# Attention into a two-layer MLP: a flag gathered behind the last matmul, the last output tile in two halves, no fillers behind transpositions

## The chip, the cores and the metric

The kernel runs on one core of a Trainium2 chip. A core has five engines that each work through a list of instructions in order and wait for one another by semaphores: TensorE (PE; its weight loads are shown apart as PEld), VectorE (DVE), ScalarE (ACT), GpSimd (POOL) and SyncE (SP, which here only starts transfers and takes branches). The metric is the device time of one execution in microseconds; lower is better.

## The reference

Attention with a causal window of 128 positions and four "sink" positions that every row sees, for 4 batches, 8 heads, 768 positions and 64 dimensions; its result, as rows of 512 per token, goes through an MLP.

```python
scores = np.matmul(q, k.transpose(0, 1, 3, 2)) / np.sqrt(D)
keep = (pos[None, :] < n_sink) | ((rel >= 0) & (rel < window))   # rel = row - column
a = softmax(np.where(keep, scores, -1e9))
x = np.matmul(a, v).transpose(0, 2, 1, 3).reshape(B * S, H * D)   # 3072 x 512
h = x @ w_in                                                       # 512 x 2048
out = np.maximum(0.01 * h, h) @ w_out                              # 2048 x 512
```

The two weights arrive as 64-bit floats, `n_sink` and `window` as 64-bit integers.

## The kernel before

The tokens are cut into NU = 8 units `u` of 384 tokens (half a batch, T = 3 tiles of 128). A unit has attention (four pairs of heads) and an MLP of NFC = 16 steps `fc`, one for each 128 of the 2048 inner columns. A step of the MLP is twelve matmuls for `h` (128x384, L511: four blocks of the inner dimension, each as three products, high with high, low with high and high with low, since both operands are split in two parts) and nine for the output of the step before (128x512, L537: three token tiles, three products each: `woh,gh`, `wol,gh`, `woh,gl`). Between them ACT makes 0.01`h` (L518), DVE the maximum `g` (L521), ACT the high part `gh` (L522), POOL the low part `gl` (L523). While a unit goes through its MLP, PE does the attention of the next unit in between.

The 16 weight tiles of each matrix come as 64-bit words. DVE turns each into a 32-bit float in three instructions of 512 columns (`di` or `do` at L166 and L168, then `wi` or `wo` at L170, with the letter i for `w_in` and o for `w_out`); ACT and POOL then make the two parts (L179, L180). The first three tiles are decoded during the attention of unit 0, the others in the MLP steps of unit 0.

PE's order is written out by hand (L570: the recorded order holds for PE alone). The order of the other engines is made by a scheduler that lays the instructions out on a modelled timeline, so it can change wherever the program changes. On PE, L253 (`keep_warm`) issues filler matmuls of 256 columns into the bank `h`, with zeros and a result that nobody reads: 17 at the start, and one behind the four transpositions of each tile of unit 0's attention (in `turn_native`, L309 to L322).

PSUM is cut into eight banks of 128x512: `s0`, `s1`, `o0`, `o1`, `o2`, `t`, `h`, `d`. The outputs of a unit are summed in `o0`, `o1`, `o2` over 16 steps. Step 1 puts its `h` into the bank `o2` (L506), so the first matmul that writes `o2` as an output has to wait until `g` of step 1 has been read from it.

The kernel is only valid for small `n_sink`, `window` and normal numbers. `needs_general` (L595 to L615) collects the conditions on DVE into one number for each partition (`one`, L609), turns them into a row on PE (`flag_t`, L610) and reduces that to a flag (L612, L614). It is called in the last unit (u = 7) in the pass of the loop for step 14, behind the outputs of step 13 and ahead of `h` of step 15. Each engine loads the flag (L749) and branches on it (L750); the general path behind the branch isn't taken with these inputs.

The last output tile is read from its bank by halves: the first 256 columns by ACT, the others by DVE (L549), each stored by its own queue (L550: ACT's and SP's). The 23 tiles before it are copied by DVE (L553) and stored on SP's queue (L554).

Of the kernel before, what the change touches and what calls it, by code (L numbers as in the profile page):

```python
# [9 lines left out]
F32 = mybir.dt.float32  # L10
# [8 lines left out]
ENG = mybir.EngineType  # L19
MANUAL = {ENG.PE}  # L20
P = 128
B, H, S, D = 4, 8, 768, 64
DM, DF = 512, 2048
# [3 lines left out]
NFC = DF // P  # L27
T = 3
NU = 2 * B
# [100 lines left out]
def fast_path(ctx, tc, cpool, qp, qk, vu, vs, wq, out, ident, lim, masks, wz, negm, wmin, wmax):  # L130
    nc = tc.nc
# [7 lines left out]
    def bank(tag, name):  # L139
        return psum.tile([P, 512], F32, tag=tag, name=name)  # L140
# [3 lines left out]
    anchor = [None]  # L144
# [38 lines left out]
    def fetch_check(n):  # L183
        k, fc = divmod(n, NFC)
        raw = iopool.tile([P, 512, 2], I32, tag="raw", name=f"craw{n}", bufs=3)
        nc.sync.dma_start(out=raw.rearrange("p f t -> p (f t)"), in_=wq[k, fc])
        checks.append((n, raw))
# [63 lines left out]
    def keep_warm(n):  # L251
        for _ in range(n):
            nc.tensor.matmul(warm[:, 0:2 * P], lhsT=wz[:, 0:P], rhs=wz, start=True, stop=True)  # L253
# [55 lines left out]
    def turn_native(u, pair, j, w, state):  # L309
        half = u % 2  # L310
        kn = KSL[half][j][1]
        tp = turn_bank(u, f"t{u}_{pair}_{j}")
        cols = (0, W1) if kn == W3 else (NSK,)
        m = P * len(cols)
        o0 = 2 * P * j if half else max(2 * j - 1, 0) * P
        for o in range(2):
            for c, a in enumerate(cols):
                nc.tensor.transpose(out=tp[:, o * m + c * P:o * m + (c + 1) * P], in_=w[:, o, a:a + P],  # L318
                                    identity=ident)
        if u == 0:  # L320
            keep_warm(1)
        nc.scalar.copy(out=state["pt"][:, :, o0:o0 + m], in_=tp[:, 0:2 * m].rearrange("p (o q) -> p o q", o=2))  # L322

    def turn_packed(u, pair, o, w, state):
# [170 lines left out]
    def mlp_stream():  # L495
        po = {}
        prev = None
        for step in range(NU * NFC + 1):
# [27 lines left out]
                yield u  # L526
            if prev is not None:
                v, f, gh, gl = prev
                if f == 0:
                    po = [bank(f"o{t}", f"o{v}_{t}") for t in range(T)]  # L530
                wh, wl = wts["o", f]
                order = [(t, c) for t in range(T) for c in range(2)] + [(t, 2) for t in range(T)]
                if f == NFC - 1 or step == 1:
                    order.sort()
                for i, (t, c) in enumerate(order):
                    tsl = slice(t * P, (t + 1) * P)
                    nc.tensor.matmul(po[t], lhsT=(gl if c == 2 else gh)[:, tsl], rhs=wl if c == 1 else wh,  # L537
                                     start=f == 0 and c == 0, stop=f == NFC - 1 and c == 2)
                    if i in (2, 5):
                        yield v  # L540
                    if f < NFC - 1 or c < 2:
                        continue
                    last = v == NU - 1 and t == T - 1
                    r0 = (v * T + t) * P
                    if last:
                        for i, (copy, queue) in enumerate(((nc.scalar.copy, nc.scalar), (nc.vector.tensor_copy, nc.sync))):
                            half = slice(256 * i, 256 * (i + 1))
                            ob = iopool.tile([P, 256], F32, tag="raw", name=f"ob{v}_{t}_{i}", bufs=3)
                            copy(out=ob, in_=po[t][:, half])  # L549
                            queue.dma_start(out=out[r0:r0 + P, half], in_=ob)  # L550
                    else:
                        ob = iopool.tile([P, 512], F32, tag="io", name=f"ob{v}_{t}", bufs=3)
                        nc.vector.tensor_copy(out=ob, in_=po[t])  # L553
                        nc.sync.dma_start(out=out[r0:r0 + P, :], in_=ob)  # L554
                yield v
            prev = cur
            if u == NU - 1 and fc == NFC - 2:
                flags.append(needs_general(tc, anchor[0], cpool, bank("t", "flag_t"), ident, lim, negm,
                                           wmin, wmax))
                tc.mark_branch_hint_location("general", engines=[ENG.PE, ENG.Activation, ENG.DVE, ENG.Pool])  # L560
            at = step - FIRST_CHECK
            if at >= 0:
                for _ in range(2 if checks else 0):
                    check_weights()
                while len(checks) < min(3, 2 * NFC - 2 * at):
                    fetch_check(2 * at + len(checks))

    steps = [NPAIR * (2 * T + 2 if native(u) else 2 * T + 4) for u in range(NU)]
    flags = []
    stream = attention_stream()  # L570
    ctx.enter_context(tc.manual_schedule(engines=MANUAL))
    done = 0
# [19 lines left out]
    return flags[0]  # L592


def needs_general(tc, after, pool, row, ident, lim, negm, wmin, wmax):  # L595
    nc = tc.nc
    bad = pool.tile([P, 6], F32, name="bad")
    deep = pool.tile([P, 1], F32, name="deep")
# [8 lines left out]
        nc.vector.tensor_scalar(out=bad[:, 3 + i:4 + i], in0=deep, scalar1=bound, scalar2=None, op0=op)  # L607
    one = pool.tile([P, 1], F32, name="one")
    nc.vector.tensor_reduce(out=one, in_=bad, axis=AX.X, op=ALU.max)  # L609
    nc.tensor.transpose(out=row[0:1, 0:P], in_=one, identity=ident)  # L610
    allp = pool.tile([1, 1], F32, name="allp")
    nc.vector.tensor_reduce(out=allp, in_=row[0:1, 0:P], axis=AX.X, op=ALU.max)  # L612
# [186 lines left out]
```

## Time and profile before

| | us |
|---|---|
| median of 3 runs | 706.63 (706.54 to 706.93) |
| the profiled execution | 705.64 |
| its span in the trace | 703.9 |
| PE busy in the span | 688.9 (98%) |
| DVE, ACT, POOL busy | 443.5, 325.9, 315.4 |

The profile is of one execution, 0.99 us under the median of the runs and with 1.74 us outside its span. Shares over the whole span say little here: PE is 98% busy, but the span has a start in which other engines work too, a long stretch of steps and an end, which have to be looked at one by one. Times in the rows are in us from the start of the span; a row with "x3" merges three instructions in a row, and the bracket behind it gives the idle time of the engine before it and what ended it. A matmul's length in the rows runs past the start of the next one, so the time that one costs in a row of matmuls is read from start to start. A "q" behind an engine's name (SPq) is its queue of instructions that aren't counted as busy.

### The profile page before, as it was taken

The numbers are of one execution on the slowest core, as the hardware profiler recorded it, in microseconds if no ns is written. First come the engines' busy times: TensorE is split into PE (matmuls) and PEld (weight loads), VectorE is DVE, ScalarE is ACT, GpSimd is POOL, SyncE is SP. The second block draws the span as 40 slices with busy tenths as digits, with TensorE's granted clock in tenths as the row PEclk, the third lists the DMA queues.
The fourth block names the chain that finished last, engine by engine and source line by source line (L and its number), as shares of the span: only waits on it lengthen the run. The fifth ranks groups of instructions, "written<-read, shape, count | busy, mean of one in ns | idle before, by whom it ended". The sixth has DMA issues, their size and how long they took to land.

```text
span 703.9 us, 11359 instructions
## 1 busy us (share of the span) xinstructions
PE 688.9 (98%) x3938; PEld 595.0 (85%) x3938; DVE 443.5 (63%) x1181; ACT 325.9 (46%) x855; POOL 315.4 (45%) x390
## 2 busy tenths in 40 slices
PE   8889999999999999999999999999999999999995
PEld 5568788889888889888888988888898888889994
DVE  5997879655566556465566655565556755377663
ACT  5865666545444444444454444444454443222221
POOL 4676776654443444444354444344444433122221
PEclk9999999999999999999999999999999999999999
DMA  6675665421223211131222222132112320068751
GB/s 222 215 241 180 194 199 174 152 67 50 80 61 116 73 53 49 59 117 51 80 80 71 77 73 69 46 114 64 59 60 80 102 71 31 1 207 281 245 179 48
DMA packets 29534, 77.28 MB, mean 110 GB/s; under 512 B 3488, under 2 KB 9120, under 8 KB 29472
## 3 DMA queue, kind: packets, MB, share of 16 engines
q1 hardware_dynamic: 29328, 76.38, 33.9%
q8 instruction: 32, 0.52, 0.3%
q14 instruction: 30, 0.25, 0.1%
q10 hardware_dynamic: 144, 0.13, 0.1%
HBM read 70.21 MB, written 6.29 MB: 109 GB/s over the span
## 4 chain that ended last, share of the span: by engine, by line
PE 90%; DVE 6%; ACT 1%; issue 1%; DMA 0%; DVEq 0%; ACTq 0%
PE h L511 37%; PE o L537 36%; PE acc L366 5%; PE s L282 5%; PE t L328 2%; PE acc L373 2%; PE s L277 1%; PE t L318 1%; ACT pk L291 1%; DVE pk L289 1%; DVE di L168 1%; DVE do L166 1%; DVE do L168 1%; DVE di L166 1%; PE sk L344 0%
## 5 line engine op out<-in xcount | busy, mean ns | idle before, releaser
L523 POOL TENSOR_TENSOR gl<-g,gh 128x384 fp32r<-128x384 f32 x127 | 136.5, 1075 | 226.3 <-ACT gh L522 222.3
L511 PE MATMUL h<-xh,wih 128*128 128x384 f32 x512 | 180.7, 353 | 0.3 <-DVE g L521 0.2
L511 PE MATMUL h<-xl,wih 128*128 128x384 f32 x512 | 172.2, 336 | 1.2 <-POOL xl L381 1.2
L511 PE MATMUL h<-xh,wil 128*128 128x384 f32 x512 | 172.4, 337 | 0.0
L537 PE MATMUL o<-wol,gh 128*128 128x512 f32 x384 | 152.9, 398 | 0.0
L537 PE MATMUL o<-woh,gh 128*128 128x512 f32 x384 | 151.6, 395 | 0.9 <-DVE g L521 0.7
L537 PE MATMUL o<-woh,gl 128*128 128x512 f32 x384 | 114.1, 398 | 0.0
L291 ACT ACTIVATE pk<-pk,negm 128x132 f32<-128x132 f32 (+1 forms) x192 | 81.5, 425 | 62.8 <-DVE negm L289 60.2
L522 ACT CAST gh<-g 128x384 fp32r<-128x384 f32 x128 | 65.7, 514 | 94.5 <-DVE g L521 94.4
L521 DVE TENSOR_TENSOR g<-h,g 128x384 f32<-128x384 f32 x128 | 71.1, 556 | 60.0 <-ACT g L518 58.3
L511 PEld LDWEIGHTS h<-xh,wih 128*128 128x128 f32 x512 | 96.3, 188 | 9.6 <-issue 2.7
L511 PEld LDWEIGHTS h<-xl,wih 128*128 128x128 f32 x512 | 96.5, 188 | 6.4 <-POOL xl L381 1.5
L243 POOL TENSOR_TENSOR qksp<-qkraw,qksp 64x396 fp32r<-64x396 f32 (+1 forms) x48 | 56.7, 1181 | 94.2 <-issue 91.1
L511 PEld LDWEIGHTS h<-xh,wil 128*128 128x128 f32 x512 | 96.0, 188 | 0.0
L518 ACT ACTIVATE g<-h 128x384 f32<-128x384 f32 x128 | 62.7, 490 | 71.6 <-PE h L511 68.4
L537 PEld LDWEIGHTS o<-woh,gh 128*128 128x128 f32 x384 | 72.2, 188 | 10.7 <-DVE g L521 1.1
L537 PEld LDWEIGHTS o<-woh,gl 128*128 128x128 f32 x384 | 69.4, 188 | 13.7 <-DVE gl L523 0.2
L537 PEld LDWEIGHTS o<-wol,gh 128*128 128x128 f32 x384 | 72.1, 188 | 8.6
L242 ACT CAST qksp<-qkraw 128x780 fp32r<-128x780 f32 (+1 forms) x48 | 43.2, 900 | 71.0 <-PE s L282 67.9
L453 DVE COPY_PREDICATED s<-tri,s 128x128 f32<-128x128 int8 x120 | 35.0, 291 | 38.7 <-PE s L282 38.7
L282 PEld LDWEIGHTS s<-qksp 128*128 128x128 f32 x288 | 53.2, 188 | 6.2
L282 PE MATMUL s<-qksp 128*128 128x260 f32 (+1 forms) x288 | 56.2, 277 | 0.0
(106 smaller groups left out, 851.2 us busy)
## 6 DMA issues: line engine op xcount, KB each, us to landing
craw<-in_wq SPq DMA_DIRECT2D x32, 512.0 KB, 4.6
qkraw<-in_qk SPq DMA_DIRECT2D x24, 454.0 KB, 3.2
qkraw<-in_qk SPq DMA_DIRECT2D x24, 390.0 KB, 3.0
wiraw<-in_wq SPq DMA_DIRECT2D x16, 512.0 KB, 3.7
woraw<-in_wq SPq DMA_DIRECT2D x16, 512.0 KB, 3.6
out<-ob SPq DMA_DIRECT2D x23, 256.0 KB, 2.7
svr<-in_vs SPq DMA_DIRECT2D x24, 192.0 KB, 2.3
v<-in_vu SPq DMA_DIRECT2D x16, 256.0 KB, 2.7
```

The lines of the kernel that those rows point to most:

```text
L242: nc.scalar.copy(out=sp[:, 0:TU + n], in_=raw[:, 0:TU + n])
L243: nc.gpsimd.tensor_tensor(out=sp[D:P, TU:TU + n], in0=raw[D:P, TU:TU + n], in1=sp[D:P, TU:TU + n].bitcast(F32), op=ALU.subtract)
L282: nc.tensor.matmul(pss[0][:, 0:kn], lhsT=sp[:, off + j * P:off + (j + 1) * P], rhs=sp[:, TU + k0:TU + k0 + kn], start=c == 0, stop=c == 1)
L291: nc.scalar.activation(out=w, in_=w, func=AF.Exp, scale=-1.0, bias=neg, accum_out=sm)
L366: nc.tensor.matmul(acc[o * D:(o + 1) * D, qo:qo + m], lhsT=vv[:, kb * P + o * D:kb * P + (o + 1) * D], rhs=state["pt"][:, o, po:po + m], s ...
L453: nc.vector.copy_predicated(out=ps[:, W1:W3], mask=late[0][1], data=ps[:, 0:P])
L511: nc.tensor.matmul(ph[:, 0:TU], lhsT=w[:, cs], rhs=x, start=cc == 0 and c == 0, stop=cc == NCC - 1 and c == 2)
L518: nc.scalar.mul(g, ph[:, 0:TU], 0.01)
L521: anchor[0] = nc.vector.tensor_tensor(out=g, in0=ph[:, 0:TU], in1=g, op=ALU.max)
L522: nc.scalar.copy(out=gh, in_=g)
L523: (nc.vector if step == NU * NFC - 1 else nc.gpsimd).tensor_tensor(out=gl, in0=g, in1=gh.bitcast(F32), op=ALU.subtract)
L537: nc.tensor.matmul(po[t], lhsT=(gl if c == 2 else gh)[:, tsl], rhs=wl if c == 1 else wh, start=f == 0 and c == 0, stop=f == NFC - 1 and c ...
```

## The change

Three edits. (a) The filler behind the transpositions of unit 0's attention is left out: 12 fillers fewer, the 17 at the start remain. (b) In the last unit, output tile 2 is summed as two halves of 256 columns, one in the bank `o2` and one in `s0`: a step has six matmuls of 512 and six of 256 columns where it had nine of 512. The first half is copied by ACT and the second by DVE, and both are stored on ACT's queue. (c) `needs_general` ends with `one`; the transposition, the reduction and the cast are in `to_flag`, called once behind the last matmul of the last unit.

```diff
@@ turn_native @@
-        if u == 0:
-            keep_warm(1)
         nc.scalar.copy(out=state["pt"][:, :, o0:o0 + m], in_=tp[:, 0:2 * m].rearrange("p (o q) -> p o q", o=2))
@@ mlp_stream @@
+                end = f == NFC - 1
                 if f == 0:
-                    po = [bank(f"o{t}", f"o{v}_{t}") for t in range(T)]
+                    po = [(t, slice(0, DM), bank(f"o{t}", f"o{v}_{t}")) for t in range(T)]
+                    if v == NU - 1:
+                        po[2:] = [(2, slice(256 * i, 256 * i + 256), bank(tag, f"o{v}_2_{i}")[:, 0:256])
+                                  for i, tag in enumerate(("o2", "s0"))]
                 wh, wl = wts["o", f]
-                order = [(t, c) for t in range(T) for c in range(2)] + [(t, 2) for t in range(T)]
-                if f == NFC - 1 or step == 1:
+                order = [(i, c) for i in range(len(po)) for c in range(2)] + [(i, 2) for i in range(len(po))]
+                if end or step == 1:
                     order.sort()
...
+                for n, (i, c) in enumerate(order):
+                    t, cols, acc = po[i]
+                    nc.tensor.matmul(acc, lhsT=(gl if c == 2 else gh)[:, t * P:(t + 1) * P],
+                                     rhs=(wl if c == 1 else wh)[:, cols], start=f == 0 and c == 0, stop=end and c == 2)
...
-                            copy(out=ob, in_=po[t][:, half])
-                            queue.dma_start(out=out[r0:r0 + P, half], in_=ob)
...
+                    if len(po) > T and i >= 2:
+                        ob = iopool.tile([P, 256], F32, tag="raw", name=f"ob{v}_{i}", bufs=3)
+                        (nc.vector.tensor_copy if i == 3 else nc.scalar.copy)(out=ob, in_=acc)
+                        nc.scalar.dma_start(out=out[rows, cols], in_=ob)
...
             if u == NU - 1 and fc == NFC - 2:
-                flags.append(needs_general(tc, anchor[0], cpool, bank("t", "flag_t"), ident, lim, negm,
-                                           wmin, wmax))
-                tc.mark_branch_hint_location("general", engines=[ENG.PE, ENG.Activation, ENG.DVE, ENG.Pool])
+                bad.append(needs_general(tc, anchor[0], cpool, lim, negm, wmin, wmax))
...
+        tc.mark_branch_hint_location("general", engines=[ENG.PE, ENG.Activation, ENG.DVE, ENG.Pool])
+        flags.append(to_flag(nc, cpool, bank("t", "flag_t"), ident, bad[0]))
@@ needs_general @@
     one = pool.tile([P, 1], F32, name="one")
     nc.vector.tensor_reduce(out=one, in_=bad, axis=AX.X, op=ALU.max)
+    return one
+
+
+def to_flag(nc, pool, row, ident, one):
     nc.tensor.transpose(out=row[0:1, 0:P], in_=one, identity=ident)
     allp = pool.tile([1, 1], F32, name="allp")
     nc.vector.tensor_reduce(out=allp, in_=row[0:1, 0:P], axis=AX.X, op=ALU.max)
```

Because the scheduler orders all engines but PE, the edits also move instructions far from the lines that they touch. On DVE, in step 1 of unit 0's MLP, this stood before (a name's last number is that of its buffer; `pk` and `negm` are the attention of unit 1, the waits in brackets name the engine or transfer queue waited for):

```order
L170 SCALAR_TENSOR_TENSOR wo_622<-woraw_615,do_623 128x512 [waits DVE_49,Pool_49]
L166 TENSOR_SCALAR di_667<-wiraw_662 128x512 [waits DMAHW3_49,DVE_49]
L289 ISA pk_1_0_691,negm<-s_2_0_687,m_86 128x260 [waits PE_49]
L289 ISA negm 128x1
L289 ISA pk_1_0_691,negm<-s_3_0_688,m_86 128x260 [waits PE_49]
L289 ISA negm 128x1
L168 SCALAR_TENSOR_TENSOR di_667<-wiraw_662,di_667 128x512 [waits DVE_49]
L170 SCALAR_TENSOR_TENSOR wi_666<-wiraw_662,di_667 128x512 [waits DVE_49,Pool_49]
L521 TENSOR_TENSOR g_1_707<-h_1_676,g_1_707 128x384 [waits Activation_49]
L166 TENSOR_SCALAR do_672<-woraw_664 128x512 [waits DMAHW5_49,DVE_49]
L168 SCALAR_TENSOR_TENSOR do_672<-woraw_664,do_672 128x512 [waits DVE_49]
L170 SCALAR_TENSOR_TENSOR wo_671<-woraw_664,do_672 128x512 [waits DVE_49,Pool_49]
```

and in the changed kernel there stands, from the same row of the engine's list on:

```order
L519 TENSOR_TENSOR g_0_628<-h_0_615,g_0_628 128x384 [waits Activation_49]
L166 TENSOR_SCALAR di_655<-wiraw_650 128x512 [waits DMAHW3_49,DVE_49]
L168 SCALAR_TENSOR_TENSOR di_655<-wiraw_650,di_655 128x512 [waits DVE_49]
L170 SCALAR_TENSOR_TENSOR wi_654<-wiraw_650,di_655 128x512 [waits DVE_49,Pool_49]
L166 TENSOR_SCALAR do_660<-woraw_652 128x512 [waits DMAHW5_49,DVE_49]
L289 ISA pk_1_0_679,negm<-s_2_0_675,m_86 128x260 [waits PE_49]
L289 ISA negm 128x1
L168 SCALAR_TENSOR_TENSOR do_660<-woraw_652,do_660 128x512 [waits DVE_49]
L289 ISA pk_1_0_679,negm<-s_3_0_676,m_86 128x260 [waits PE_49]
L289 ISA negm 128x1
L170 SCALAR_TENSOR_TENSOR wo_659<-woraw_652,do_660 128x512 [waits DVE_49,Pool_49]
L519 TENSOR_TENSOR g_1_695<-h_1_664,g_1_695 128x384 [waits Activation_49]
```

`g_0` is now behind `wo` of its weight tile instead of ahead of it, and `g_1` is behind the three instructions that decode the next `w_out` tile (`do` twice, `wo`), which followed it before.

On PE, in the last unit behind the outputs of step 13, the transposition of the flag stood between the last output matmul and the first of `h_15`:

```order
L537 MATMUL o_1_6996<-woh_1428,gl_13_7431 128x512
L537 MATMUL o_2_6997<-woh_1428,gl_13_7431 128x512
L610 MATMUL flag_t<-ident,one 1x128 [waits DVE_49,PE_49]
L511 MATMUL h_15_7497<-xh_0_6216,wih_1561 128x384
L511 MATMUL h_15_7497<-xl_0_6217,wih_1561 128x384
L511 MATMUL h_15_7497<-xh_0_6216,wil_1562 128x384
```

In the changed kernel the end of PE's list is this; `o_2_0` and `o_2_1` are the two halves:

```order
L539 MATMUL o_1_6984<-woh_1553,gh_15_7533 128x512
L539 MATMUL o_1_6984<-wol_1554,gh_15_7533 128x512
L539 MATMUL o_1_6984<-woh_1553,gl_15_7534 128x512
L539 MATMUL o_2_0_6986<-woh_1553,gh_15_7533 128x256
L539 MATMUL o_2_0_6986<-wol_1554,gh_15_7533 128x256
L539 MATMUL o_2_0_6986<-woh_1553,gl_15_7534 128x256
L539 MATMUL o_2_1_6987<-woh_1553,gh_15_7533 128x256
L539 MATMUL o_2_1_6987<-wol_1554,gh_15_7533 128x256
L539 MATMUL o_2_1_6987<-woh_1553,gl_15_7534 128x256
L613 MATMUL flag_t<-ident,one 1x128 [waits PE_49]
L752 TENSOR_LOAD flag [waits DVE_49]
```

The transposition has moved behind the last matmul, and it no longer waits for DVE there but for PE itself.

On SP the last stores and the flag stood so:

```order
L749 TENSOR_LOAD flag [waits DVE_49]
L749 ISA x2
L554 DMA out<-ob_0_7529 128x512 [waits DVE_49]
L554 DMA out<-ob_1_7535 128x512 [waits DVE_49]
L550 DMA out<-ob_2_1_7544 128x256 [waits DVE_49]
L750 COMPARE_AND_BRANCH
```

and stand so now:

```order
L553 DMA out<-ob_0_7554 128x512 [waits DVE_49]
L553 DMA out<-ob_1_7560 128x512 [waits DVE_49]
L752 TENSOR_LOAD flag [waits DVE_49]
L752 ISA x2
L753 COMPARE_AND_BRANCH
```

The flag's load has moved behind the stores, and the third store has gone to ACT's queue.

## Rows read from the trace of the kernel before

**Rows 1.** The page's part 4, the chain's shares by engine.

```profile
PE 90%; DVE 6%; ACT 1%; issue 1%; DMA 0%; DVEq 0%; ACTq 0%
```

**Rows 2.** Stretches: length; busy PE, PEld, DVE, ACT, POOL (count); clock, DMA, GB/s.

```profile
15.70:44.80 29.10, 25.30 (x170) 17.02 (x170) 27.99 (x82) 23.00 (x66) 21.45 (x40) 1.00 0.68 232
44.80:60.00 15.20, 15.20 (x91) 11.76 (x91) 12.29 (x27) 9.19 (x22) 11.76 (x14) 1.00 0.73 220
```

**Rows 3.** Timeline of PE at 44.8 us: start, length, engine, line, operation.

```profile
44.79 0.50 PE L537 MATMUL o<-woh,gh 128*128 128x512 f32 x1 [0.70 <-DVE g L521]
```

**Rows 4.** Timeline of DVE, 44 to 47 us.

```profile
44.19 0.55 DVE L521 TENSOR_TENSOR g<-h,g 128x384 f32<-128x384 f32 x1
44.65 0.68 DVE L166 TENSOR_SCALAR do<-woraw 128x512 int32<-128x512 int32 x1
45.37 0.69 DVE L168 SCALAR_TENSOR_TENSOR do<-woraw,do 128x512 int32<-128x512 int32 x1
46.17 0.69 DVE L170 SCALAR_TENSOR_TENSOR wo<-woraw,do 128x512 int32<-128x512 int32 x1
```

**Rows 5.** Timeline of PE, a filler in the first unit.

```profile
11.84 0.27 PE L253 MATMUL warm<-wz 128*128 128x256 bf16 x1
12.05 0.71 PE L277 MATMUL s<-qkn 64*128 64x260 f32 x4
```

**Rows 6.** Timeline of PE, the steps around the flag's transposition.

```profile
683.09 0.39 PE L537 MATMUL o<-woh,gh 128*128 128x512 f32 x1
...
685.18 0.34 PE L511 MATMUL h<-xh,wih 128*128 128x384 f32 x1
...
687.26 0.39 PE L537 MATMUL o<-woh,gh 128*128 128x512 f32 x1
...
690.39 0.27 PE L610 MATMUL flag_t<-ident,one 128*1 128x128 f32 x1 [0.87 <-DVE one L609]
...
692.58 0.39 PE L537 MATMUL o<-woh,gh 128*128 128x512 f32 x1
```

**Rows 7.** Timeline of PE, a pair of 260 columns and what follows.

```profile
251.32 0.40 PE L282 MATMUL s<-qksp 128*128 128x260 f32 x2
251.56 0.34 PE L511 MATMUL h<-xh,wih 128*128 128x384 f32 x1
```

**Rows 8.** Timeline of all engines, the last copies and stores.

```profile
695.65 1.38 DVE L553 COPY ob<-o 128x512 f32<-128x512 f32 x2 [0.60 <-PE o L537]
...
696.37 2.17 SPq L554 DMA_DIRECT2D out<-ob  x2
...
696.61 0.40 PE L537 MATMUL o<-woh,gl 128*128 128x512 f32 x1
...
697.45 0.43 DVE L549 COPY ob<-o 128x256 f32<-128x256 f32 x1 [0.41 <-ACT ob L549]
698.58 0.43 SPq L550 DMA_DIRECT2D out<-ob  x1
```

**Rows 9.** Instructions on the output tiles, last 14 us: duration in ns min/median/max.

```profile
L554 SPq DMA_DIRECT2D out<-ob x2: 347/910/1473, 696.4 to 697.1; - x2
```

**Rows 10.** Instructions of the branch's line: duration in ns, first and last start.

```profile
L750 SPq EVENT_SEMAPHORE  x8: 17/17/17, 702.0 to 702.6; - x8
...
L750 SPq COMPARE_BRANCH  x1: 50/50/50, 699.1 to 699.1; - x1
```

**Rows 11.** Timeline of DVE, the flag's reduction and cast.

```profile
690.69 0.28 DVE L612 TENSOR_REDUCE allp<-flag_t 1x1 f32<-1x128 f32 x1 [0.45 <-PE flag_t L610]
691.01 0.14 DVE L614 CAST flag<-allp 1x1 int32<-1x1 f32 x1
```

**Rows 12.** Instructions of the flag's load on SP.

```profile
L749 SPq TENSOR_LOAD <-flag x1: 469/469/469, 691.2 to 691.2; - x1
...
L749 SPq FUSED_REGOPS  x1: 186/186/186, 691.7 to 691.7; - x1
```

**Rows 13.** Groups of PE's weight loads by line: busy us, mean ns.

```profile
L537 PEld LDWEIGHTS o<-woh,gh 128*128 128x128 f32 x384 | 72.2, 188 | 10.7 <-DVE g L521 1.1 <-DVE ob L553 0.9
```

More of the change, by code (lines that the diff above doesn't have):

```diff
@@ L533, in mlp_stream @@
-                if f == NFC - 1 or step == 1:
+                order = [(i, c) for i in range(len(po)) for c in range(2)] + [(i, 2) for i in range(len(po))]
+                if end or step == 1:
                     order.sort()
[L535 to L539, printed above, removed]
+                for n, (i, c) in enumerate(order):
+                    t, cols, acc = po[i]
+                    nc.tensor.matmul(acc, lhsT=(gl if c == 2 else gh)[:, t * P:(t + 1) * P],
+                                     rhs=(wl if c == 1 else wh)[:, cols], start=f == 0 and c == 0, stop=end and c == 2)
+                    if n in (2, 5):
@@ L540, in mlp_stream @@
                         yield v
-                    if f < NFC - 1 or c < 2:
+                    if not end or c < 2:
                         continue
[L543 to L548, printed above, removed]
-                            copy(out=ob, in_=po[t][:, half])
-                            queue.dma_start(out=out[r0:r0 + P, half], in_=ob)
+                    rows = slice((v * T + t) * P, (v * T + t + 1) * P)
@@ L551, in mlp_stream @@
+                    if len(po) > T and i >= 2:
+                        ob = iopool.tile([P, 256], F32, tag="raw", name=f"ob{v}_{i}", bufs=3)
+                        (nc.vector.tensor_copy if i == 3 else nc.scalar.copy)(out=ob, in_=acc)
+                        nc.scalar.dma_start(out=out[rows, cols], in_=ob)
                     else:
                         ob = iopool.tile([P, 512], F32, tag="io", name=f"ob{v}_{t}", bufs=3)
-                        nc.vector.tensor_copy(out=ob, in_=po[t])
@@ L554, in mlp_stream @@
-                        nc.sync.dma_start(out=out[r0:r0 + P, :], in_=ob)
+                        nc.vector.tensor_copy(out=ob, in_=acc)
+                        nc.sync.dma_start(out=out[rows, :], in_=ob)
                 yield v
@@ L566, in mlp_stream @@
                     fetch_check(2 * at + len(checks))
+        tc.mark_branch_hint_location("general", engines=[ENG.PE, ENG.Activation, ENG.DVE, ENG.Pool])
+        flags.append(to_flag(nc, cpool, bank("t", "flag_t"), ident, bad[0]))
     steps = [NPAIR * (2 * T + 2 if native(u) else 2 * T + 4) for u in range(NU)]
-    flags = []
+    flags, bad = [], []
     stream = attention_stream()
@@ L592, in fast_path, with needs_general @@
     return flags[0]
-def needs_general(tc, after, pool, row, ident, lim, negm, wmin, wmax):
+def needs_general(tc, after, pool, lim, negm, wmin, wmax):
     nc = tc.nc
```

## The prediction, made before the result was known

> **What bounds the kernel now.** I read the page's shares first, then the stretches, then the timelines of the engine that binds in each stretch. The chain of work that ended last is TensorE (PE) for 90% of the span and VectorE (DVE) for 6% [rows 1]. The stretches show that this is two regimes. From 15.7 to 44.8 us PE is busy 25.30 of 29.10 us and DVE 27.99, so DVE, which decodes the weights and takes part in the first unit's attention, sets the pace; from 44.8 to 60 us PE is busy 15.20 of 15.20 [rows 2]. The last wait of the first regime is the matmul at 44.79, which waited 0.70 us for DVE's `g` [rows 3]. What is lost before it stays lost, since PE has no idle time behind it to win it back; what is saved on DVE behind it saves nothing. Near the end one stall is left (the flag's), then the tail: the last copies, the stores, and SP's branch.
>
> **The change part by part.** All terms are made against the profiled execution, 705.64 us, which is 0.99 us under the median of the runs, 706.63; I add their sum to the median.
>
> *The start: +2.1.* The scheduler's new order puts three decoding steps (`do` L166, `do` L168, `wo` L170) ahead of step 1's `g`, on DVE. Before, `g` began at 44.19 and the three ran behind it, starting at 44.65, 45.37 and 46.17, the last for 0.69 [rows 4]. That is 0.72 + 0.80 + 0.69 = 2.21; an instruction may begin a little before its predecessor ends, as 44.65 against the end of `g` (44.19 + 0.55) shows, so I take 2.1, bounds 1.8 and 2.4. Step 1's `h` stands in the bank that output tile `o_2` needs, so the matmul that began at 44.79 [rows 3] now begins near 46.9. DVE was the bound up to there, so nothing else can hide it, and the three instructions done early bring no return: behind them PE waits for nobody [rows 2]. `g` of step 0 is one decoding step later too (0.7), and so are `gh` and `gl`; the six matmuls ahead of `o_2` then start later, but the later wait swallows theirs. Upstream, a reciprocal now stands behind one score instruction, and other neighbours are swapped; I give it nothing, ±0.3.
>
> *The fillers: 0.* One filler held PE for 0.21 us, from 11.84 to 12.05 [rows 5]. There are 12 fewer, up to 2.5 us of PE time, but it lies in stretches in which PE waits anyway (3.8 us idle from 15.7 to 44.8 alone, [rows 2]); at most 0.1 of it shows on a chain that feeds DVE, which is inside the ±0.3. What binds next there is DVE, unchanged.
>
> *The flag out of the last unit: −1.15.* In an undisturbed step the nine output matmuls take from 683.09 to 685.18 (2.09) and the twelve of `h` from 685.18 to 687.26 (2.08). The disturbed step began its outputs at 687.26 and without a stall would begin the next outputs at 687.26 + 2.09 + 2.08 = 691.43; it began them at 692.58 [rows 6]. The transposition that waited for `one` on DVE, and the `h` queued behind it, cost 1.15. `one` is computed where it was, its result just isn't waited for until the last matmul is through, seven us later. What is late next in that step: the output matmuls wait for `g` as in every step. Bounds −0.9 (the idle time that the row itself names) and −1.2.
>
> *The halves: +0.2.* The last unit sums tile 2 by 96 matmuls of 256 columns where 48 of 512 stood. Nothing of 256 columns in float runs here before; the nearest are the pairs of 260 columns, which take from 251.32 to 251.56, 0.24 for two with different weights [rows 7]. The wide ones take 2.09 / 9 = 0.232 each [rows 6]. So 96 × 0.118 − 48 × 0.232 = 11.3 − 11.1 = +0.2; the pair's 0.24, read to two places, leaves 0.1175 to 0.1225 for one, and the wide ones scaled to 256 columns give 0.116, so I take 0.118. Bounds: 0 (at 0.116) and +0.6 (at 0.1225); a half held by its own weight load is a rival below.
>
> The Trainium skill ("TensorE: Matmul & The Clock Gate", Part 3, "The mechanism") states that a weight load overlaps running matmuls only where its row group differs; in its section on LDWEIGHTS a load of 128 columns takes about 107 ns. By that rule the 48 added loads would cost an estimated 5.1 us and the sum would be +5.8 in place of +0.8. The trace speaks against it: by the rule a wide matmul would show its load on top, and the rows' 0.232 leaves no place for one.
>
> *The tail: −0.3.* Before, the flag was loaded in the middle of the last unit and SP reached its branch at 699.1, behind a slow store issue (two issues of 347 and 1473 ns) and a third at 698.58; SP went on at 702.0 [rows 8 to 10]. Now the flag is behind everything. Two halves take the place of one wide matmul, so in before's times the last half starts near 696.61 + 0.12, `flag_t` 0.12 behind it, and 0.27 on, near 697.1, it is done. DVE has two wide copies (695.65, 1.38 together, to 697.03), then the second half's copy (0.43, [rows 8]) to 697.48, the reduction (0.28), and the cast, 0.32 later and 0.14 long [rows 11], to 697.95. Loading it and the register check behind (0.47 and 0.19, [rows 12]) make some 0.7 until the branch: 698.7 against 699.1, −0.4; if the slow issue recurs the flag's load stands behind it: 698.53 + 0.7, +0.15. I take −0.3. Behind the waiting load on SP there is only its branch; on the others the program's end. Behind the branch SP needs 2.9 us (699.1 to 702.0), which I leave. Bounds: if it is the stores that SP waits for there, the last one is issued at 697.5 instead of 698.58, −1.1; if both issues are slow, 696.37 + 2 × 1.47 + 0.7 = 700.0, +0.9. That ACT and DVE now copy from two banks saves DVE's 0.41 wait for ACT [rows 8], which is in these times.
>
> Sum: 2.1 + 0 − 1.15 + 0.2 − 0.3 = +0.85; 705.64 becomes 706.5, and the median 706.63 becomes **707.5 us**.
>
> **The rivals.**
> - *The start isn't lost.* The `g` delay would have to be absorbed before PE, for instance by DVE being earlier by as much when it gets there. For it: 1.1 us of the DVE-bound stretch is idle on DVE [rows 2]. Against it: the three instructions need 2.2 us, and PE waited for exactly this `g`. Then 707.5 − 2.1 = 705.4, and with the tail bound by stores 704.6, which is faster.
> - *The halves are paced by their weight load* (slower). Place: the last unit's output matmuls. Price: 96 × 0.188, the duration of a load [rows 13], is 18.0 in place of 11.3, +6.7, giving 714.2. It decides from a pitch of about 0.124 on, where the total passes +1.4. For it: a half has half the time to cover the same load. Against it: the 260-column pairs take 0.24 for two [rows 7].
> - *The flag's chain comes late at the end.* Slow store issues ahead of the load on SP, +0.9 in place of −0.3: 708.7, slower. For it: one of the two issues was slow. Against it: the other of the two took 347 ns [rows 9], and one slow issue alone costs 0.45 over the forecast, not 1.2.
> - *PE's clock.* Fillers gone, PE could drop to 1.2 GHz in the first unit. The granted clock is 1.00 (2.4 GHz) in both stretches, with waits on PE in the first [rows 2]. If a quarter of the 25.30 us ran at half clock, 6.3 more us of work against 3.8 us idle: +2.5, 710.0.
>
> The skill's Part 1 of the same page says that an idle TensorE falls back to its slow level, which would put the time there; the first stretch with its PE idle time at full granted clock doesn't show it, and no run so far has the fillers left out.
>
> **How the numbers follow.** A measurement of this kernel tells from no change what is beyond about 0.2%, 1.4 us. Forecast 0.60 (its own range 706.2 to 708.9, from the bounds added up in part: start ±0.3, flag +0.25, tail −0.8 to +1.2, halves −0.2 to +0.4); the start not lost 0.15 (705.4); halves by weight load 0.10 (709 to 714); late flag 0.10 (708.7); clock 0.05 (710.0). Faster by over 0.2%, under 705.2: half of the second case and a little of the first, 0.11. Slower, over 708.0: the last three and a fifth of the first, 0.37. Within: 0.52. The range runs from 705.2 to 709.0; it leaves out the halves' and the clock's upper ends and the lowest of the second case.
>
> **What would show each step.** The `o` matmul that began at 44.79 begins near 46.9, with a wait of over 2 us for `g` ahead of it: right; under 45.5: the start's step fails. PE then without a wait to 687 or so, shifted by that amount. No idle time between outputs and `h` in the last two steps, h to outputs 2.08: the flag's step. The last unit's steps still 4.17 to 4.20 us long; over 4.3 means the halves cost. SP's branch at last matmul + 2.1 and its restart 2.9 later: the tail's. A granted clock under 1.00 or fillerless matmuls at twice their duration between 8 and 45 us would be the clock's.

## The result

| | before | changed |
|---|---|---|
| median, us (6 runs each) | 706.00 (705.43 to 706.93) | 710.58 (709.98 to 711.77) |
| the profiled execution | 705.64 | 711.44 |
| its span | 703.9 | 709.7 |
| granted clock, mean of the span | 0.998 | 0.991 |

The changed kernel is slower: 1.0061 times the time of before (95% interval 1.0044 to 1.0079), some 4.6 us. The forecast was 707.5 in a range of 705.2 to 709.0, so even the range missed it. The base of the forecast, 706.63, was a median of three runs; with three more it is 706.00, and beside the experiments below the same kernel has 705.5 to 705.6, so about 1 us of the base is spread.

Where the time went is read by laying the same matmul of both traces side by side (start in us from the span's start):

| the same matmul of PE | before | changed | shift | gained or lost since the row above |
|---|---|---|---|---|
| a score of unit 0 (L277) | 30.57 | 32.14 | +1.57 | +1.57 |
| first matmul of `o_2`, step 1 | 44.79 | 48.49 | +3.70 | +2.13 |
| the next score of unit 1 (L277) | 47.17 | 52.45 | +5.28 | +1.58 |
| an output matmul, start of the last unit | 628.03 | 633.27 | +5.24 | −0.04 |
| outputs of step 13, last unit | 687.26 | 693.13 | +5.87 | +0.63 |
| outputs of step 14, last unit | 692.58 | 697.38 | +4.80 | −1.07 |
| end of the span | 703.9 | 709.7 | +5.8 | +1.0 |

The +2.13 and the −1.07 are the forecast's two large terms (+2.1, −1.15). What it hadn't: two losses of 1.6 us that stand right beside falls of the clock, a tail of the wrong sign, and somewhat more for the halves.

The stretches of the changed kernel (length; busy PE, PEld, DVE, ACT, POOL with counts; granted clock, DMA share, GB/s; the third as in [rows 2]), and behind them two of before:

```profile
10.00:11.00 1.00, 0.12 (x1) 0.13 (x2) 0.67 (x4) 1.00 (x7) 0.49 (x3) 1.00 1.02 403
11.30:14.50 3.20, 3.20 (x14) 1.93 (x12) 0.96 (x5) 1.72 (x7) 0.59 (x4) 0.52 0.13 51
44.80:60.00 15.20, 12.70 (x60) 10.00 (x61) 11.14 (x28) 8.62 (x23) 9.08 (x13) 0.89 0.60 186
49.00:52.30 3.30, 3.30 (x12) 2.72 (x11) 2.11 (x4) 1.14 (x3) 2.41 (x3) 0.50 0.70 191
```

```profile
10.00:11.00 1.00, 0.55 (x3) 0.28 (x2) 0.70 (x4) 1.00 (x7) 0.51 (x3) 1.00 1.01 398
11.00:15.00 4.00, 4.00 (x32) 2.36 (x31) 1.27 (x9) 3.65 (x12) 1.00 (x5) 1.00 0.46 157
```

PE is busy throughout 11.3 to 14.5 and 49.0 to 52.3, but at a granted clock of 0.52 and 0.50: about the 1.2 GHz level in place of 2.4. Before, the clock was 1.00 from 11 to 15 us and in both stretches of [rows 2]. In the microsecond ahead of the first fall PE is busy for 0.12 us, where it was 0.55 before. The timeline of PE at the first fall, the same place before, and the second fall (it answers to [rows 3]):

```profile
10.88 0.75 PE L277 MATMUL s<-qkn 64*128 64x260 f32 x2 [0.89 <-DVE sm L302]
11.55 1.11 PE L318 MATMUL t<-ident,pk 128*128 128x128 f32 x4
12.60 1.24 PE L277 MATMUL s<-qkn 64*128 64x260 f32 x4
```

```profile
10.72 0.70 PE L277 MATMUL s<-qkn 64*128 64x260 f32 x2 [0.45 <-DVE sm L302]
11.35 0.66 PE L318 MATMUL t<-ident,pk 128*128 128x128 f32 x4
```

```profile
45.80 0.50 PE L539 MATMUL o<-woh,gl 128*128 128x512 f32 x1 [1.07 <-POOL gl L521]
...
48.49 0.50 PE L539 MATMUL o<-woh,gh 128*128 128x512 f32 x1 [1.50 <-DVE g L519]
...
50.27 0.67 PE L509 MATMUL h<-xh,wih 128*128 128x384 f32 x1
```

Ahead of the first fall PE sat idle 0.89 us for `sm`; the four transpositions behind it take 1.05 up to the next start (11.55 to 12.60), where the same four took 0.49 in before (11.35 to 11.84). Ahead of the second it waited twice, 1.07 us for `gl` of step 0 and 1.50 for `g` of step 1, and the `h` of step 2 then started 1.78 behind the first `o_2` matmul, where it was 1.15 before. The timeline of DVE, with the three decoding steps now ahead of `g` (answers to [rows 4]):

```profile
45.39 0.69 DVE L166 TENSOR_SCALAR do<-woraw 128x512 int32<-128x512 int32 x1
...
46.34 0.69 DVE L168 SCALAR_TENSOR_TENSOR do<-woraw,do 128x512 int32<-128x512 int32 x1
...
47.28 0.68 DVE L170 SCALAR_TENSOR_TENSOR wo<-woraw,do 128x512 int32<-128x512 int32 x1
47.88 0.55 DVE L519 TENSOR_TENSOR g<-h,g 128x384 f32<-128x384 f32 x1
```

`do` begins at 45.39, the score instruction and `do` L168 follow, `wo` at 47.28, `g` at 47.88. The end of the kernel, by the chain (start, length, what):

```profile
691.17 2.13 PE h L509 x12
693.30 2.11 PE o L539 x12
695.41 2.13 PE h L509 x12
```

Twelve matmuls with halves take 2.11, nine wide ones took 2.09 by [rows 6], and no flag stands between outputs and `h`. The twelve of `h`, which the edit leaves as they were, take 2.13 in every step from 642 us on; in the last unit of before they took 2.08 and 2.12 by turns. Last, the flag and the branch: the timeline, the loads of the flag, and the branch's line (they answer to [rows 8, 10, 12]):

```profile
701.54 0.28 PE L539 MATMUL o<-woh,gl 128*128 128x256 f32 x1
...
701.65 0.27 PE L613 MATMUL flag_t<-ident,one 128*1 128x128 f32 x1
...
702.49 0.14 DVE L617 CAST flag<-allp 1x1 int32<-1x1 f32 x1
```

```profile
L752 SPq TENSOR_LOAD <-flag x1: 927/927/927, 702.7 to 702.7; - x1
...
L752 DVEq TENSOR_LOAD <-flag x1: 997/997/997, 702.7 to 702.7; - x1
```

```profile
L753 SPq EVENT_SEMAPHORE  x8: 17/17/17, 707.8 to 708.4; - x8
...
L753 SPq COMPARE_BRANCH  x1: 50/50/50, 704.0 to 704.0; - x1
```

Five engines load the flag at 702.7 to 702.8 and branch at 703.7 to 704.0. A load takes 0.87 to 1.00 us in place of 0.47 ([rows 12]), and SP goes on 3.8 us behind its branch (704.0 to 707.8) in place of 2.9.

### The profile page after: what moved, and what is told of

It is laid out like the page before. It is cut to its first block, busy times and chain, and to the rows that moved or that the text cites. A ratio compares the mean times of both kernels' runs of the same rounds, so it can differ in the third digit from the quotient of the medians.

```text
span 709.7 us, 11431 instructions
## 1 busy us (share of the span) xinstructions
PE 691.4 (97%) x3974; PEld 599.5 (84%) x3974; DVE 443.7 (63%) x1181; ACT 325.8 (46%) x855; POOL 315.4 (44%) x390
## 4 chain that ended last, share of the span: by engine, by line
PE 90%; DVE 6%; ACT 2%; issue 1%; DMA 0%; DVEq 0%; ACTq 0%
PE h L509 37%; PE o L539 36%; PE acc L364 5%; PE s L282 5%; PE t L326 2%; PE acc L371 2%; PE s L277 1%; ACT pk L291 1%; PE t L318 1%; DVE pk L289 1%; DVE do L166 1%; DVE di L168 1%; DVE do L168 1%; PE sk L342 0%; DVE g L519 0%
## 5 line engine op out<-in xcount | busy, mean ns | idle before, releaser
L539 PE MATMUL o<-woh,gh 128*128 128x512 f32 (+1 forms) x400 | 153.7, 386 | 1.7 <-DVE g L519 1.5
L539 PE MATMUL o<-wol,gh 128*128 128x512 f32 (+1 forms) x400 | 154.5, 389 | 0.0
L539 PE MATMUL o<-woh,gl 128*128 128x512 f32 (+1 forms) x400 | 114.7, 389 | 1.1 <-POOL gl L521 1.1
L539 PEld LDWEIGHTS o<-woh,gh 128*128 128x128 f32 x400 | 75.3, 188 | 11.3 <-DVE g L519 1.9
L539 PEld LDWEIGHTS o<-woh,gl 128*128 128x128 f32 x400 | 71.4, 188 | 14.4 <-POOL gl L521 1.5
L539 PEld LDWEIGHTS o<-wol,gh 128*128 128x128 f32 x400 | 75.1, 188 | 8.7
```

What stands on the lines that cost most here:

```text
L539: nc.tensor.matmul(acc, lhsT=(gl if c == 2 else gh)[:, t * P:(t + 1) * P], rhs=(wl if c == 1 else wh)[:, cols], start=f == 0 and c == 0, s ...
```

## The experiments

All ratios are to the kernel before, run beside them; each median is of 5 to 12 runs, and that of before was 705.5 to 705.6 in all of them. The texts of what was expected count the runs in another order, that in which they went on record: their first is 1 here, their third 6, their tenth 7 and their eleventh 11.

**1. Only the fillers left out.**

```diff
-        if u == 0:
-            keep_warm(1)
```

> The kernel before with only the twelve fillers behind unit 0's transpositions left out. Theory (the fillers' removal is what makes the change slow, by the scheduler's order and by PE's clock): the matmul that waits for g of step 1 begins some 3.7 us later than in the kernel before, granted clock 0.5 for some 3 us after 11 us and again after 49 us, time +3.6 to +5.3 us against the kernel before. Rival (the fillers are hidden, the loss is in the end of the kernel): within 0.3 us of the kernel before.

Measured: 710.36 us (707.64 to 714.28), ratio 1.0067 (1.0041 to 1.0092). The whole loss comes with this edit alone. Its stretches, and its matmul of `o_2`:

```profile
10.00:11.00 1.00, 0.15 (x1) 0.15 (x2) 0.66 (x4) 1.00 (x7) 0.52 (x3) 0.99 1.01 402
11.00:15.00 4.00, 4.00 (x14) 2.19 (x14) 1.09 (x5) 2.12 (x7) 0.86 (x4) 0.50 0.16 62
15.00:18.00 3.00, 3.00 (x18) 1.71 (x16) 0.49 (x4) 1.40 (x5) 0.88 (x3) 0.53 0.45 133
44.80:60.00 15.20, 12.40 (x67) 9.33 (x64) 12.39 (x30) 9.16 (x24) 10.46 (x14) 1.00 0.62 197
```

```profile
50.31 0.50 PE L535 MATMUL o<-woh,gh 128*128 128x512 f32 x1 [1.74 <-DVE g L519]
```

PE, busy 0.15 us in the eleventh microsecond, then ran some 7 us at 0.50 to 0.53; the wait for `g` came as in the changed kernel (1.74), but the clock stayed at 1.00 behind it. So the fall at 49 us is not bound to happen. One edit, a spread of 6.6 us: the fastest run, with a mean clock of 0.998 as before has it, is 2.1 us over before, which fits the late `g` without any fall; it has no trace.

**2. The changed kernel with the fillers back** (the two lines above put back).

> The changed kernel with the twelve fillers put back; flag and halves as changed. Theory: the order on VectorE at the start is that of before, the clock stays at 1.00 in all stretches up to the end, and what is left is the flag -1.1, the halves +0.6 and the tail +0.9: +0.4 us against the kernel before, so about 4 us faster than the changed kernel. Rival (the loss is in the end): +4 us against before, as the changed kernel.

Measured: 706.47 us, ratio 1.0010 (1.0001 to 1.0019): +0.9. The clock is 1.00 in every microsecond up to 60 us. So the rest of the change is a small loss, and the rival fails. It is twice the +0.4 expected: by 14 us the matmuls of this profile are 0.3 us behind those of before; why was not followed up.

**3. Fillers only behind the first pair.**

```diff
-        if u == 0:
+        if u == 0 and pair == 0:
             keep_warm(1)
```

> The kernel before with fillers only behind the three transpositions of unit 0's first pair (three in place of twelve); VectorE's order at step 1 is then that of the changed kernel (g behind the three decoding steps). Theory: the clock stays full from 8 to 45 us, so the first stretch costs nothing, g late costs 2.1, and a fall of the clock after 49 us, where it comes, 1.5 more: +2.1 to +3.6. Rival (three fillers don't keep the clock up, or the clock isn't theirs): +4.8 as without any.

Measured: 709.07 us (707.79 to 710.26), ratio 1.0047 (1.0033 to 1.0062), +3.5. Its stretches:

```profile
10.00:11.00 1.00, 0.55 (x3) 0.29 (x2) 0.72 (x4) 1.00 (x7) 0.62 (x3) 1.00 1.00 395
11.00:15.00 4.00, 4.00 (x32) 2.46 (x31) 1.35 (x7) 3.54 (x11) 0.98 (x6) 1.00 0.47 164
...
44.80:60.00 15.20, 13.72 (x66) 10.94 (x65) 11.18 (x28) 9.41 (x24) 8.44 (x14) 0.89 0.51 169
```

Three fillers keep PE at 0.55 us busy in the eleventh microsecond and the clock at 1.00 behind it; the fall after the wait for `g` still comes (0.89 over 44.8 to 60). The nine fillers that are gone cost nothing and won nothing: the matmul that began at 10.72 in before begins 0.11 earlier in this profile, and the one that began at 41.91 begins 0.13 earlier. The order on DVE in step 1 is that of the changed kernel, so the loss is the late `g` (2.2 us by the trace) and one fall (1.6).

**4. The same, with PE kept busy while it waits.**

```diff
                 for i, (t, c) in enumerate(order):
+                    if step == 1 and i in (2, 6):
+                        bridge = bank("h", f"bridge{i}")
+                        for _ in range(9 if i == 2 else 14):
+                            nc.tensor.matmul(bridge[:, 0:2 * P], lhsT=wz[:, 0:P], rhs=wz, start=True, stop=True)
```

> The experiment with three fillers, and besides 9 and 14 fillers of 256 columns on PE ahead of the two output matmuls of step 1 that wait for gl and for g, so that PE is busy while it waits. Theory: g is as late as before the bridge (+2.1 us), but no run shows a granted clock of 0.5 after 45 us: +2.1 to +2.5 us with little spread. Rival (the clock falls there for another reason, or the fillers delay the matmuls behind them): +2.5 to +4.

Measured: 707.75 us (four of six runs between 707.60 and 707.79), ratio 1.0037 (1.0024 to 1.0049), +2.2. The last fillers and the first `o_2` matmul, and the stretch behind:

```profile
45.24 1.70 PE L539 MATMUL bridge<-wz 128*128 128x256 bf16 x14
46.88 0.50 PE L541 MATMUL o<-woh,gh 128*128 128x512 f32 x1
```

```profile
44.80:60.00 15.20, 15.20 (x90) 11.66 (x90) 12.66 (x31) 9.88 (x26) 9.83 (x15) 1.00 0.65 193
```

The `o_2` matmul begins at 46.88 (44.79 before), the place that the forecast named, and the clock stays at 1.00. So the late `g` costs 2.1 by itself. Against experiment 3 the fall behind the wait is 1.3 on top by the medians and 1.5 by the traces. That PE's idling brings this fall is likely but not shown: the two kernels' runs overlap (the other two here took 709.15 and 709.46, without a trace), and experiment 1 has the idling without the fall.

**5. No fillers, but `g` ahead again.**

```diff
+                first = ("i",) if step == 1 else ("i", "o")
...
-                    load_weights(new)
+                    load_weights(new, first)
...
-                    round_weights(new)
+                    round_weights(new, first)
                 anchor[0] = nc.vector.tensor_tensor(out=g, in0=ph[:, 0:TU], in1=g, op=ALU.max)
+                if step == 1:
+                    load_weights(new, ("o",))
+                    round_weights(new, ("o",))
```

> No fillers behind transpositions, as in the first experiment, but the w_out tile of step 1 decoded behind g of step 1 (as it stood in the kernel before); nothing else changed. Theory (two separate costs: VectorE's order, and PE's clock after too long a pause): the wait for g of step 1 is at most 0.8 us again and the clock stays full after 45 us, the fall of the clock after 11 us stays: +1.3 to +3 us against the kernel before, 2 to 3 less than without fillers alone. Rival (the order is not what delays PE, the clock alone does it): +4.8 as without fillers alone.

Measured: 710.88 us (706.90 to 711.83), ratio 1.0058 (1.0039 to 1.0077), +5.3, against the expectation of +1.3 to +3. Its stretches, and its output matmuls of step 1:

```profile
15.00:25.00 10.00, 9.97 (x44) 5.75 (x40) 5.41 (x21) 4.00 (x15) 2.90 (x8) 0.50 0.19 62
44.80:60.00 15.20, 13.62 (x72) 10.24 (x71) 13.49 (x31) 9.90 (x26) 10.31 (x14) 1.00 0.63 190
```

```profile
49.54 0.50 PE L539 MATMUL o<-woh,gl 128*128 128x512 f32 x1 [1.06 <-POOL gl L525]
...
51.27 0.50 PE L539 MATMUL o<-woh,gh 128*128 128x512 f32 x1 [0.53 <-DVE g L520]
```

The edit did half of what was expected. The wait for `g` of step 1 is 0.53 us and no fall follows; but `g` of step 0 still stands behind the decoding of its tile on DVE, and its `gl` behind `wol` of that tile on POOL, which it preceded in before. So `gl` is as late as in experiment 1 (a wait of 1.06), and that costs 1.2 us: against before, PE is 5.3 us late ahead of these matmuls and 6.5 behind them. The 5.3 come with the first fall, 3 us long in the changed kernel and 13 in this profile. The expectation had taken the length of a fall from two profiles; it can't be had from them. The fastest run, 706.90 with a mean clock of 0.998, is 1.4 over before, about the price of `gl`. But three others, 710.87 to 710.95, have a mean clock of 0.998 too, so a fall as in the profiled run (711.83, mean clock 0.989) isn't seen in them; what made those three slow stays open.

**6. Only the flag behind the last matmul** (its function split and its second half moved as in the change).

> The kernel before with only the flag gathered behind the last matmul; fillers kept, last tile summed and stored as before. Theory (five engines loading the flag at the same moment make the load take 0.9 us and SP's branch 3.8 instead of 2.9): the stall of 1.1 us in the last unit goes and the tail gets 0.9 to 1.1 us longer, so -0.2 to +0.1 us. Rival (the longer tail comes from the halves and the single queue): -1.1 us.

Measured: 705.62 us, ratio 1.0003 (0.9994 to 1.0012). The stall goes (the `h` of step 15 starts 1.06 sooner relative to the steps ahead) and comes back in the tail. The rival, that the halves made the tail longer, fails: there are none here.

**7. The same with SP named in the branch hint.**

```diff
-        tc.mark_branch_hint_location("general", engines=[ENG.PE, ENG.Activation, ENG.DVE, ENG.Pool])
+        tc.mark_branch_hint_location("general", engines=[ENG.PE, ENG.Activation, ENG.DVE, ENG.Pool, ENG.SP])
```

> The kernel with only the flag gathered behind the last matmul (third experiment), and SP named in the branch hint too. Theory (five engines that branch at the same moment fetch at the same moment, and SP, which has no hint, waits longest, 3.7 us): SP's pause falls by over 1 us and the time by 0.4 to 1 us against the third experiment (so 704.6 to 705.2 us where before has 705.5). Rival (the load of 0.75 us and the pause come from all engines reading the flag at once, a hint on SP doesn't matter): no change.

Measured: 702.55 us, ratio 0.9959 (0.9945 to 0.9974): −3.0 against before and −3.1 against experiment 6. The branch's line on SP in 6 and in 7:

```profile
L755 SPq EVENT_SEMAPHORE  x8: 17/17/17, 701.9 to 702.4; - x8
...
L755 SPq COMPARE_BRANCH  x1: 50/50/50, 698.2 to 698.2; - x1
```

```profile
L755 SPq EVENT_SEMAPHORE  x8: 17/17/17, 698.8 to 699.3; - x8
...
L755 SPq COMPARE_BRANCH  x1: 70/70/70, 698.3 to 698.3; - x1
```

The pause behind SP's branch was 3.7 us (698.2 to 701.9) and is 0.5 (698.3 to 698.8). The theory had the place right and the size three times too small. How much a shorter pause can win is told by the stores behind it: in experiment 6 the last of them was issued at 696.7 and landed 2.0 us later, 3.2 us ahead of the pause's end.

**8. The transposition behind the sixth output matmul of step 14** instead of at the end (before is otherwise unchanged), and **9. that with SP in the hint.**

```diff
+                    if v == NU - 1 and f == NFC - 2 and i == 5:
+                        flags.append(to_flag(nc, cpool, bank("t", "flag_t"), ident, bad[0]))
+                        tc.mark_branch_hint_location("general", engines=[ENG.PE, ENG.Activation, ENG.DVE, ENG.Pool])
```

> The kernel before with the transposition of the flag issued behind the sixth output matmul of step 14 in the last unit, where its operand on VectorE has been ready for over 2 us, and the load of the flag ahead of the stores as before. Theory: the stall goes and the tail stays, -1.1 us against before. Rival (the stall only moves to the next wait, such as that for g of step 15): 0.

> The kernel with the flag's transposition behind the sixth output matmul of step 14, and SP named in the branch hint besides the other four engines. Theory (SP's pause of 2.8 to 2.9 us between its branch and its next instruction is the fetch of instructions at the branch's target, which the other engines have had hinted): the pause falls to about 0.5 to 1 us, the landing of the last store, some 3 us after its issue, then ends the kernel: -0.2 to -0.6 us against that kernel without the hint on SP. Rival (the pause is the wait for the stores): no change.

Measured: 704.57 us, ratio 0.9980 (0.9969 to 0.9991), −1.0; and 704.00, ratio 0.9980 (0.9970 to 0.9990), some −1.5 by the medians. The stall could be saved without the late flag. Here the hint on SP was worth 0.5 by the medians and nothing by the ratios, which is not clear of noise. The branch's line on SP in experiment 9, then transfers from 695.5 to 698.6 us in experiment 9 and in experiment 7 (share of the engines, then KB each and time from issue to landing):

```profile
L756 SPq EVENT_SEMAPHORE  x8: 17/17/17, 700.2 to 700.8; - x8
...
L756 SPq COMPARE_BRANCH  x1: 70/70/70, 697.9 to 697.9; - x1
```

```profile
q8 instruction: 1, 0.02, 2.1%
q14 instruction: 2, 0.02, 2.0%
...
out<-ob SPq DMA_DIRECT2D x2, 256.0 KB, 3.8
out<-ob ACTq DMA_DIRECT2D x1, 128.0 KB, 3.8
out<-ob SPq DMA_DIRECT2D x1, 128.0 KB, 3.5
```

```profile
q1 hardware_dynamic: 432, 0.66, 58.8%
...
out<-ob SPq DMA_DIRECT2D x2, 256.0 KB, 2.1
```

With the early flag the engines branch one by one while the last stores are under way, and three instruction transfers lie in that stretch beside stores that take 3.8 us; with the late flag there is none there, and the stores take 2.1. That the one causes the other was not tested. The pause of 2.2 us that is left in experiment 9 is the wait for the stores, as its expectation had it: SP's first instruction behind the branch starts at 700.18, and ACT's store, issued at 696.38, lands 3.8 us later at 700.16; SP's next starts at 700.37, and the last store lands at 700.35. In experiment 8 the last store lands at 701.8, only 0.4 ahead of the pause's end at 702.25, so a shorter pause had little to win there.

**10. Only the halves**, as changed, fillers and flag as before.

> The kernel before with only the last unit's third output tile summed in two halves in two banks, both stored on ScalarE's queue; flag and fillers as before. Theory: the last unit's steps get 0.04 us longer each (4.22 in place of 4.18), +0.6 in all; the tail changes by -0.5 to 0, as the two copies no longer wait for one another and SP has two stores instead of three: +0.1 to +0.6 us. Rival (halves held by their weight load, the price of my forecast's rival): +6.7. Rival two (the single queue costs the tail more than it saves): over +0.9.

Measured: 706.18 us, ratio 1.0009 (0.9996 to 1.0022), +0.6. PE loses 0.62 us from 630 to 687 us, as in the changed kernel; the tail doesn't pay it back. Half of the 0.62 lies in the outputs (2.11 us a step in place of 2.09) and half in `h` (2.13 in every step in place of 2.08 and 2.12 by turns). The rival of the weight load (+6.7) fails.

**11. A version for both ends.** The transposition as in 8, SP hinted, fillers kept, and the whole weight tile of step 1 decoded behind `g`. **12.** The same with the flag at the end as in 7.

```diff
-                if u == 0 and new < NFC:
+                if u == 0 and new < NFC and step != 1:
                     load_weights(new)
...
+                if step == 1:
+                    load_weights(new)
+                    round_weights(new)
                 nc.scalar.copy(out=gh, in_=g)
```

> A version against both kernels: fillers kept, the flag's transposition behind the sixth output matmul of step 14, SP in the branch hint, and the weight tile of step 1 (both matrices) decoded behind g of step 1, so that g comes some 2 us sooner than in the kernel before. Theory: the wait of 0.7 us at 44.8 us goes, or most of it, on top of the 1.5 us that the two edits at the end gave: -1.7 to -2.2 us against the kernel before. Rival (another wait takes the place of g, such as gl of step 0 on GpSimd, or the weights come too late for step 4): -1.5 us or less.

> The version that the runs point to: the fillers kept, the flag gathered behind the last matmul with SP named in the branch hint (the tenth experiment), and step 1's weight tile decoded behind g of step 1 (the start of the eleventh). Theory: the two gains lie at opposite ends of the kernel and add up, -3.0 - 0.7 = -3.7 us against the kernel before, near 701.9 us. Rival (a part of the end's gain was luck of the stores' issues): -2.2 to -3 us.

Measured: 703.36 us, ratio 0.9969 (0.9958 to 0.9980), and **702.01 us, ratio 0.9949 (0.9933 to 0.9966)**, 3.5 under before and 8.6 under the changed kernel's median (not run beside it). In 11 the first `o_2` matmul:

```profile
43.61 0.40 PE L540 MATMUL o<-woh,gl 128*128 128x512 f32 x1
44.08 0.50 PE L540 MATMUL o<-woh,gh 128*128 128x512 f32 x1
```

The wait of 0.70 is gone, and the later matmuls, up to the last unit, are 0.68 to 0.70 earlier than in before. The median is 2.2 under before, as expected. The gains of both ends add up as expected, within 0.2.

## Why the prediction was wrong, step by step

- **The start, +2.1: right.** `o_2` starts 2.13 later than the shift that it found, and at 46.88 with nothing else wrong (experiment 4). One reading on the way was off: `gl` of step 0 comes 1.7 later against the shift (44.74 on POOL, 41.48 before) and not 0.7, since POOL now makes `wol` ahead of it. The wait for `g` takes that in; where `g` is early (experiment 5), the late `gl` alone costs 1.2. The forecast worked it out of DVE's order and [rows 4], and PE didn't make it up again: the shift stays within 0.04 from 47 to 628 us.
- **The fillers, 0: this is the step that failed.** They were priced as PE work that lies in idle time and so is free, with the clock as a rival at 0.05 and +2.5. The work is free (experiment 3: nine of twelve gone, and at 42 us nothing won or lost by it); the idle time that is left without it isn't. Without fillers PE's busy share in the eleventh microsecond went from 0.55 to between 0.12 and 0.15, and behind it the clock fell to its lower level in all three profiles without these fillers (for 3 to 13 us), and in none of the eleven with three or twelve. In the changed kernel this cost 1.6 us. It is the sign that the forecast had named for the clock, a granted clock under 1.00 between 8 and 45 us. The rival's 710.0 lies near the measured 710.58 by luck: it had 2.5 us in the first unit and no second fall. [rows 5] showed a filler between transpositions and scores, and PE awaits `sm` just ahead (0.45 us, the row of 10.72 above); I asked what the filler costs and not what PE did in its place. The profile of before had no fall in unit 0 to price it from: the fillers were in it.
- **What a wait costs besides itself.** The second fall came after the waits for `gl` and `g`, 1.6 us on top of the 2.13, in the changed kernel and in experiment 3, not in experiment 1. The forecast took a wait of PE as the time until its matmul starts. In experiment 4 `g` is as late, PE isn't idle and no fall comes, so the late `g` alone doesn't bring it; that the idling does was argued, since experiment 1 had the idling and no fall.
- The Trainium skill ("TensorE: Matmul & The Clock Gate", Part 1, "What's actually happening") says that an idle TensorE goes back to half its clock. I weighed that rule and left it at one chance in twenty because the first stretch of [rows 2] had idle time at full clock. The changed kernel's stretches, 0.52 and 0.50, agree with the page on that level.
- **An order instruction underrated.** The reciprocal that moved behind one score instruction was given ±0.3. In the changed profile PE waits 0.89 us for `sm`, where it waited 0.45; with the filler gone too, that is the pause ahead of the first fall: PE gets there 0.27 sooner and `sm` comes 0.16 later than before. How much each of the two does to the clock was not tried apart.
- **The flag, −1.15: right** (−1.07 with one more step of halves in it, 0.04).
- **The halves, +0.2: too small, +0.6.** Starts of halves lie 0.118 to 0.127 apart in the trace, 0.12 on average, inside the bounds given (0.1175 to 0.1225), and by the forecast's own sum that makes +0.4. What it left out is `h`: its twelve matmuls beside halves take 2.13 in every step, where they took 2.08 and 2.12 by turns, another 0.3 or so over the unit. Why stays open.
- **The tail, −0.3: wrong sign, +1.0.** The chain up to the cast went as worked out (0.95 from the last start to the cast at 702.49; the forecast's numbers give 1.08). The load took 0.93 and not 0.47, and SP's pause behind the branch 3.8 and not 2.9: "which I leave", the forecast said of it. It carried the 2.9 over without asking what it is. The third rival had the price (+0.9) with another mechanism; the store issues were quick, 0.34 each. Experiments 6 and 7 show that with the late flag most of the pause is SP's missing hint: naming SP in it takes 3.2 of 3.7 us away. Why the load and the pause are longer with the late flag was not tested.

## What to carry to other kernels

Work that an engine does in its idle time can be free and still be needed: before taking fillers out, ask what the engine's clock will be in the pauses that remain, and price a fall from a run without them, since the profile with them can't show it. A scheduler that orders engines by a modelled timeline moves instructions far from the edit, so read the new order first at the place where the bound engine hands over. And when a pause stands in every profile, as SP's 2.7 to 3.8 us behind an unhinted branch, ask what it is before leaving it: with the flag at the end, naming SP in the hint was worth 3.1 us. First ask what ends next behind the pause, since that bounds the gain: 3.2 us to the landing of the stores there, 0.4 with the early flag.

## What the runs showed that was not expected

The length of a fall of the clock varied from one kernel to the next and from run to run: some 3, 7 and 13 us by the profiles of the changed kernel, experiment 1 and experiment 5, and 707.64 to 714.28 us for one kernel.

The profiled execution of experiment 8 took 705.98 us where that kernel's median is 704.57, and its trace shows a wait at the start of the last unit that is 0.2 us in the other profiles (1.1 in that of the twelfth experiment):

```profile
632.43 0.69 DVE L194 TENSOR_REDUCE wmax<-craw 128x1 f32<-128x512 f32 x1 [1.48 <-DMA craw<-in_wq]
...
634.36 0.50 PE L537 MATMUL o<-woh,gh 128*128 128x512 f32 x1 [1.73 <-DVE ob L556]
```

DVE waited 1.48 us for a weight tile that is read again for the check of its range (`craw`), with the copies of the unit's outputs queued behind that check, and PE waited 1.73 us for those copies to free its bank. No run tested a cure for it.
